# Loads and stores of 90-row tiles cut into a block of 64 rows at partition 32 and a small rest

## The chip, the cores and the metric

The kernel runs on one core of a Trainium2 chip. The metric is the device time of one execution in microseconds; a lower time is better. A core has five engines that run their own instruction streams beside each other: TensorE (PE, with its weight loads PEld), VectorE (DVE), ScalarE (ACT), GpSimd (POOL) and SyncE (SP). Here SP does nothing but issue transfers between the chip's main memory and the on-chip memory of 128 partitions; the transfers run on sixteen DMA engines.

## The reference

A long convolution of `x` (8 batches, 5696 positions, 128 channels) with `h`, done by a Fourier transform of twice the length, is followed by a "soft mixture of experts" over all 45568 tokens:

```python
Xf = np.fft.rfft(x, n=2*S, axis=1); Hf = np.fft.rfft(h, n=2*S, axis=0)
y = np.fft.irfft(Xf * Hf[None], n=2*S, axis=1)[:, :S].reshape(B*S, D)
logits = y @ phi                                   # 32 slots
d = softmax over tokens;  slot_input = d.T @ y     # 32 x 128
slot_out = relu(slot_input @ w1[e]) @ w2[e]        # 8 experts, 4 slots each
out = softmax over slots(logits) @ slot_out
```

## The kernel before, in words

The convolution is a transform in two factors, N1 = 90 and N2 = 64, all in float32 matrix products. The 5696 positions are 89 rows (R1) of 64. The work runs in 92 steps over one list written out by hand (`for t in range(steps)`), in which four stages of different batches stand beside each other. The filter `h` goes first as group 0, then the eight batches of `x`.

- Stage A, steps 0 to 71, eight steps per group. `load_x` (L157) brings 89 rows of `x` into a tile `xc` (a ring of three), three steps ahead. `fold` (L174, POOL) adds and subtracts its two halves into `x0` and `x1`. `stage_a` (L183) multiplies by the table `s1` (L190, PE), ACT copies two results into the tile `fst` (L192, three buffers), and SP stores 90 rows of it to main memory as F (L195). There are two F stores a step.
- Stage B, from step 9. `load_g` (L201) reads F back in another order, as 128 rows, four units ahead (`gt`, five buffers; 23 units per group, three a step). PE multiplies by `wt` (L220), DVE by the transformed filter (L238 to L244), PE by `vt` (L256); ACT copies into `zst` (L259, three buffers), and SP stores it as z (L261). For the filter, ACT and DVE keep the results on the chip instead (L227 to L232). The tables `wt` and `vt` are loaded in pieces during steps 7 to 22 (L525).
- Stage C, from step 26, one pair of tiles every two steps. `load_z` (L281) reads z back as 90 rows into `zc` (a ring of two, four near the end; the two added ones are called `zd`). PE multiplies by the table `i1` (L308), DVE and POOL fold (L314 to L324), PE transposes (L331), and the logits, the running softmax over tokens and the weighted sums follow (L341 to L424). A step's softmax weights go to main memory (L452).
- The tail, after the last step: the experts, and then the output, 25 stores of up to 1 MB (L696 to L713).

SP works in program order: an F store that waits for ACT holds back all transfers after it. Its transfers use eight semaphores in turn, and each waits until the transfer eight places before it has landed.

Only part of the 128 partitions holds data in these tiles, and the tables are padded to match. `SPLIT` is 80, so an x load is one transfer of 80 rows and one of 9; the other two are single transfers of 90 rows. The offsets are constants:

```python
SPLIT = R1 // 16 * 16
Z0, X0, F0 = 20, 20, 19
```

The rest of `xc` and `zc` is set to zero once, so unused rows add nothing to a product.

Of the kernel before, what the change touches and what calls it, by code (L numbers as in the profile page):

```python
# [14 lines left out]
PSUM = bass.MemoryType.PSUM  # L15


def transform_tables(S, N1, N2, CH, Z0, X0, F0):

    N, R1, HALF, P = N1 * N2, S // N2, N2 // 2, 2 * N2
    k1 = np.arange(N1)  # L30
    alpha = np.pi * (k1 + 0.5) / N1
    m1 = np.arange(R1) - (N1 - 1) / 2
    a1 = np.outer(m1, alpha)
    s1 = np.stack([np.cos(a1), -np.sin(a1), -np.cos(a1)], 1)
    a0 = np.outer(alpha, np.arange(N1 // 2) + 0.5)
    i1 = np.stack([np.cos(a0), -np.sin(a0), -np.cos(a0)], 1)
    s1 = np.pad(s1, [(X0, P - R1 - X0), (0, 0), (F0, P - N1 - F0)])
    i1 = np.pad(i1[np.arange(N1).reshape(2, N1 // 2).T.reshape(-1)],
                [(Z0, P - N1 - Z0), (0, 0), (0, N2 - N1 // 2)])
    k2 = np.arange(N2)  # L40
    omega = np.pi * (k1[:, None] + 2 * N1 * k2[None] + 0.5) / N
    m2 = np.arange(HALF) - (N2 - 1) / 2
    a2 = m2[None, :, None] * omega[:, None, :]
    w = np.concatenate([np.cos(a2), np.sin(a2)], 1)
    NP = N1 // 2
    back = np.arange(N2).reshape(2, HALF // CH, CH).transpose(1, 0, 2).reshape(-1)
    wbd = np.zeros((2 * N2, NP, 2 * N2))
    vbd = np.zeros((2 * N2, NP, 2 * N2))
    for par in range(2):
        r = slice(par * N2, (par + 1) * N2)  # L50
        wbd[par::2, :, r] = w[par * NP:(par + 1) * NP].transpose(1, 0, 2)
        vbd[r, :, r] = w[par * NP:(par + 1) * NP][:, back].transpose(2, 0, 1)
    turn = (N1 - 1) / 2 * alpha[:, None] + (N2 - 1) / 2 * omega
    tn = np.zeros((2 * N2, 2, NP))
    for par in range(2):
        r = slice(par * N2, (par + 1) * N2)
        tn[r, 0] = np.cos(turn[par * NP:(par + 1) * NP]).T / N
        tn[r, 1] = np.sin(turn[par * NP:(par + 1) * NP]).T / N
    return [np.ascontiguousarray(t, dtype=np.float32) for t in (s1, i1, wbd, vbd, tn)]
# [3 lines left out]
def kernel(  # L63
# [24 lines left out]
    nc = tc.nc  # L88
    P = 128
    B, S, D = x.shape  # L90
# [4 lines left out]
    N1, N2 = 90, 64  # L95
    R1, HALF, NP = S // N2, N2 // 2, N1 // 2
    CH = 4
# [5 lines left out]
    HP = P // 2  # L103
    NQ = NJ // 2
    assert S == R1 * N2 and R1 == N1 - 1 and D == P and CH == Q == 4
    SPLIT = R1 // 16 * 16
    Z0, X0, F0 = 20, 20, 19
    ctx.enter_context(tc.manual_schedule())

    t_s1, t_i1, t_w, t_v, t_turn = [  # L110
        nc.inline_tensor(t, f"tab_{n}").ap()
        for n, t in zip(("s1", "i1", "w", "v", "turn"), transform_tables(S, N1, N2, CH, Z0, X0, F0))]
    fd = [nc.dram_tensor(f"f_{g}", (N2, N1, 2, D), F32, kind="Internal").ap() for g in range(B + 1)]
    zd = [nc.dram_tensor(f"z_{b}", (NP, 2 * N2, 2, D), F32, kind="Internal").ap() for b in range(B)]
    cd = nc.dram_tensor("c_t", (P, B * NQ, Q, 2, MH), F32, kind="Internal").ap()
# [7 lines left out]
    i1 = const.tile([P, 3, HP], F32, name="i1")  # L123
# [16 lines left out]
    s1 = apool.tile([P, 3, P], F32, name="s1", tag="s1", bufs=1)  # L140
    wt = fconst.tile([P, NP, P], F32, name="wt")
    vt = fconst.tile([P, NP, P], F32, name="vt")
    turn = fconst.tile([P, 2, NP], F32, name="turn")
# [3 lines left out]
    def bank():  # L147
        return ps.tile([P, 512], F32, name="bank", tag="bank")
# [8 lines left out]
    def load_x(c):  # L157
        if c >= (B + 1) * NJ:
            return
        g, j = divmod(c, NJ)  # L160
        src = (h if g == 0 else x[g - 1]).rearrange("(a n) d -> a n d", n=N2)
        t_ = xcs[c % len(xcs)]
        gap = N2 - CH * (2 * j + 1)
        for r in (slice(0, SPLIT), slice(SPLIT, R1)):
            v = src[r, CH * j:CH * (j + 1), :]
            v = bass.AP(tensor=v.tensor, offset=v.offset,
                        ap=[v.ap[0], [gap * D, 2], [1, CH * D]])
            nc.sync.dma_start(
                out=t_[X0 + r.start:X0 + r.stop, :, :, :].rearrange("p s n d -> p s (n d)"), in_=v)
        xs[c] = t_  # L170
# [12 lines left out]
    def stage_a(c, comp):  # L183
        g, j = divmod(c, NJ)
        src = folded.pop((c, comp))
        tab = (0, 1) if comp == 0 else (1, 2)
        st = apool.tile([P, CH, 2, D], F32, name="fst", tag="fst", bufs=3)
        for G in range(2):
            p = bank()
            nc.tensor.matmul(p[:, :], s1[:, tab[G], :],  # L190
                             src[:, :, :].rearrange("p n d -> p (n d)"), start=True, stop=True)
            nc.scalar.activation(st[:, :, G, :],  # L192
                                 p[:, :].rearrange("p (n d) -> p n d", d=D), AF.Copy)
        n0 = comp * HALF + CH * j
        nc.sync.dma_start(out=fd[g][n0:n0 + CH, :, :, :].rearrange("n k g d -> k n (g d)"),  # L195
                          in_=st[F0:F0 + N1, :, :, :].rearrange("k n g d -> k n (g d)"))


    gs, prods = {}, {}
# [81 lines left out]
    def load_z(c):  # L281
        b, j = divmod(c, NJ)
        t_ = zring.pop(0)
        zring.append(t_)
        w_ = 2 * CH * 2 * D
        nc.sync.dma_start(
            out=t_[Z0:Z0 + N1, :, :, :, :].rearrange("k o n c d -> k (o n c d)"),
            in_=zd[b].rearrange("q (a r) c d -> (q a) (r c d)",
                                a=2)[:, j * w_:(j + 1) * w_])
        zs[c] = t_  # L290

    def load_pair(T):
        if T < NT:
            load_z(2 * T)
            load_z(2 * T + 1)
# [186 lines left out]
    loaded = 0  # L482

    load_x(0)
    nc.scalar.dma_start(out=s1[:, :, :], in_=t_s1)
    for c in range(1, 3):
        load_x(c)
# [8 lines left out]
    for t in range(steps):  # L496
# [31 lines left out]
        if t < NA:  # L528
            load_x(t + 3)
            stage_a(t, 0)  # L530
            fold(t + 1, 0)
# [16 lines left out]
        if t < NA:  # L548
            stage_a(t, 1)
            fold(t + 1, 1)  # L550
# [13 lines left out]
        if t == last_front:  # L564
# [5 lines left out]
            for i in range(2):  # L570
                t_ = last.tile([P, 2, CH, 2, D], F32, name=f"zd{i}")
# [7 lines left out]
        if e > 0:  # L579
            if landed:  # L580
                place_all(*landed.pop(0))
            if kept:
                n = min(NQ, len(kept))
# [3 lines left out]
        if 0 <= i < E // 2:  # L587
            nc.sync.dma_start(
                out=w2s[:, 2 * i:2 * i + 2, :, :],
                in_=moe_w2[2 * i:2 * i + 2].rearrange("e (p c) d -> p e c d", p=P))  # L590
# [6 lines left out]
    for q in range(Q):  # L597
        r = slice(q * NSL, (q + 1) * NSL)
        nc.vector.tensor_copy(out=rep4[r, :, :],
                              in_=ident[r, r].unsqueeze(1).broadcast_to([NSL, Q, NSL]))  # L600
    p = bank()
# [5 lines left out]
    p = bank()  # L607
# [7 lines left out]
    p = bank()  # L615
# [8 lines left out]
    p = bank()  # L624
# [12 lines left out]
    for g in range(EG):  # L637
        for f0 in range(0, F, FH):
            p = bank()
# [4 lines left out]
            src = p[:, :].rearrange("p (c k) -> p k c", k=NFC)  # L644
# [5 lines left out]
    for g in range(EG):  # L650
        for k0 in range(0, NFC, 4):
            p = bank()
            for k in range(4):
# [3 lines left out]
                out=hidT[:, g, k0:k0 + 4, :], in_=p[:, :].rearrange("p (k c) -> p k c", k=4))  # L657
# [9 lines left out]
    p = bank()  # L667
# [18 lines left out]
    for b in range(B):  # L686
        for w0 in range(0, NV, G4):
            n = min(G4, NV - w0)
# [10 lines left out]
            for q in range(Q):  # L699
                dst = o_[:, 0:n + lone, q, :]  # L700
                src = pq[q][:, 0:(n + lone) * D].rearrange("p (k d) -> p k d", d=D)
# [6 lines left out]
                out=ov[b, t0:t0 + n * RW * N2, :].rearrange("(w p n) d -> p w (n d)", p=P, n=CH),  # L708
                in_=o_[:, 0:n, :, :].rearrange("p w q d -> p w (q d)"))
            if lone:  # L710
                nc.sync.dma_start(
                    out=ov[:, NV * RW * N2:, :].rearrange("b (j n) d -> b j (n d)", n=CH),
                    in_=o_[:, n, :, :].rearrange("p q d -> p (q d)"))  # L713
# [29 lines left out]
```

## Time and profile before

| what | value |
|---|---|
| median of 4 runs | 1124.95 us (1119.29 to 1127.17) |
| the profiled execution | 1119.29 us, its span 1117.4 us |
| busy: PE, PEld, DVE, ACT, POOL | 980.1, 614.6, 718.4, 517.1, 365.7 us |
| DMA engines | 78.0% busy for the main queue, 247 GB/s mean |
| mean granted TensorE clock | 0.943 |
| F stores / x loads / z loads | 144 of 360 KB / 72 of 320 KB and 72 of 36 KB / 64 of 720 KB |

The profile is one execution, taken by the hardware profiler. Busy time counts an engine's work, not its waiting; its share is a mean over stages with different limits. The chain follows the work that ended last back through what released each step, and so tells which engine or transfer set the time. A stretch's row gives the busy time of each engine between two times, the granted clock, the mean busy share of the sixteen DMA engines and GB/s. In SP's rows, the duration is the issue of a transfer alone; its landing comes later.

### The profile page before, as it was taken

The page shows a single profiled execution, that of the slowest core. Times are in us where ns is not written, and L with a number is a line of the kernel's source. Part 1 is how long each engine was busy: PE and PEld are TensorE (multiplying, and loading weights), DVE is VectorE, ACT ScalarE, POOL GpSimd, SP SyncE. Part 2 cuts the span into 40 slices and gives each one's busy share as a digit, 9 for nine tenths or more (in the row PEclk, how much of TensorE's full clock was granted, in tenths as well). Part 3 has the DMA queues.
Part 4 walks back from the last instruction along what each step waited for, and adds up shares of the span by engine and source line. Part 5 has one row for each costly group of instructions (what it writes and reads, how often), then busy time and mean ns, then how long its engine had stood idle before and what let it go on. Part 6 is the DMA issues. An engine that isn't in the chain of part 4 may idle for free.

```text
span 1117.4 us, 17250 instructions
## 1 busy us (share of the span) xinstructions
PE 980.1 (88%) x5690; PEld 614.6 (55%) x5690; DVE 718.4 (64%) x1384; ACT 517.1 (46%) x1049; POOL 365.7 (33%) x340
## 2 busy tenths in 40 slices
PE   7688898999999999999999999999997888686884
PEld 2354565555555555555555555555554555354683
DVE  2044565677777767776777677767777878565442
ACT  4477344445545444554555444444443333244332
POOL 5433222333333333333333333333331112276000
PEclk9899899999999999999999999999999999787855
DMA  7999898978788777777787778877776775764399
GB/s 204 301 275 278 290 325 267 307 252 258 231 254 252 242 232 246 250 243 231 240 248 249 232 236 249 254 227 242 246 222 190 250 253 170 210 201 164 121 381 339
DMA packets 175110, 275.49 MB, mean 247 GB/s; under 512 B 12864, under 2 KB 115776, under 8 KB 169263
## 3 DMA queue, kind: packets, MB, share of 16 engines
q1 hardware_dynamic: 174447, 274.04, 78.0%
q8 instruction: 46, 0.75, 0.3%
q10 hardware_dynamic: 576, 0.36, 0.1%
q14 instruction: 41, 0.34, 0.1%
HBM read 145.95 MB, written 128.39 MB: 246 GB/s over the span
## 4 chain that ended last, share of the span: by engine, by line
PE 65%; DVE 19%; DMA 10%; issue 2%; ACT 1%; SPq 1%; POOL 1%; DVEq 0%; ACTq 0%; POOLq 0%
PE bank L190 16%; PE bank L256 12%; PE bank L220 11%; PE bank L308 11%; PE bank L331 6%; DVE y L324 4%; DMA out_dram<-o 4%; DMA gt<-f 3%; DVE y L323 3%; PE ap L417 3%; PE bank L341 2%; DVE om L315 2%; DVE op L314 2%; DVE pi L238 2%; DVE pr L238 2%
## 5 line engine op out<-in xcount | busy, mean ns | idle before, releaser
L179 POOL TENSOR_TENSOR x<-xc 128x512 f32<-128x512 f32 x144 | 187.1, 1300 | 336.6 <-PE bank L190 314.8
L190 PE MATMUL bank<-x,s 128*128 128x512 f32 x576 | 276.8, 609 | 7.8 <-POOL x L179 7.8
L259 ACT ACTIVATE zst<-bank 128x512 f32<-128x512 f32 (+1 forms) x184 | 108.3, 588 | 347.0 <-PE bank L256 278.6
L256 PE MATMUL bank<-yf,vt 128*128 128x256 f32 x720 | 190.1, 386 | 67.3 <-DVE yf L244 63.0
L220 PE MATMUL bank<-gt,wt 128*128 128x256 f32 x810 | 220.7, 395 | 18.8 <-DMA gt<-f 18.5
L220 PEld LDWEIGHTS bank<-gt,wt 128*128 128x128 f32 x810 | 145.6, 192 | 114.1 <-issue 50.3
L192 ACT ACTIVATE fst<-bank 128x512 f32<-128x512 f32 x288 | 168.5, 598 | 72.7 <-PE bank L190 57.9
L238 DVE TENSOR_TENSOR pr<-bank,Hr 128x512 f32<-128x512 f32 (+1 forms) x184 | 124.2, 675 | 109.1 <-PE bank L220 109.1
L256 PEld LDWEIGHTS bank<-yf,vt 128*128 128x128 f32 x720 | 134.2, 191 | 102.3 <-issue 71.2
L190 PEld LDWEIGHTS bank<-x,s 128*128 128x128 f32 x576 | 108.9, 194 | 95.9 <-issue 62.9
L238 DVE TENSOR_TENSOR pi<-bank,Hi 128x512 f32<-128x512 f32 (+1 forms) x184 | 122.8, 667 | 0.0
L308 PE MATMUL bank<-zc,i 128*64 128x512 f32 x480 | 118.7, 610 | 3.9 <-DMA zc<-z 3.9
L242 DVE TENSOR_TENSOR yf<-pr,pi 128x256 f32<-128x256 f32 (+1 forms) x184 | 78.5, 427 | 6.4
L406 POOL TENSOR_TENSOR L<-L,rs 128x512 f32<-128x512 f32 x32 | 33.5, 1048 | 133.3 <-DVE rs L405 133.3
L331 PE MATMUL bank<-ident,y 128*128 128x128 f32 x512 | 69.0, 294 | 9.2 <-DVE y L324 9.2
L244 DVE TENSOR_TENSOR yf<-pr,pi 128x256 f32<-128x256 f32 (+1 forms) x184 | 75.8, 412 | 0.0
L351 DVE TENSOR_REDUCE mx<-lt 64x1 f32<-64x360 f32 x64 | 33.2, 518 | 64.4 <-ACT lt L345 63.5
L331 PEld LDWEIGHTS bank<-ident,y 128*128 128x128 f32 x512 | 65.0, 154 | 13.3 <-issue 10.6
L332 ACT ACTIVATE yt<-bank 128x360 f32<-128x360 f32 x128 | 56.2, 471 | 34.6 <-PE bank L331 34.6
L229 DVE SCALAR_TENSOR_TENSOR Hr<-bank,turn,pr 128x128 f32<-128x128 f32 x45 | 15.7, 349 | 74.3 <-ACT pr L227 74.3
L308 PEld LDWEIGHTS bank<-zc,i 128*64 128x64 f32 x480 | 29.6, 137 | 55.6 <-issue 53.5
L378 POOL MEMSET dt<- 64x8 f32 x32 | 3.4, 106 | 173.4 <-ACT dn L381 98.6
(97 smaller groups left out, 997.9 us busy)
## 6 DMA issues: line engine op xcount, KB each, us to landing
f<-fst SPq DMA_DIRECT2D x144, 360.0 KB
gt<-f SPq DMA_DIRECT2D x198, 256.0 KB
z<-zst SPq DMA_DIRECT2D x176, 256.0 KB
zc<-z SPq DMA_DIRECT2D x60, 720.0 KB
xc<-in_x_dram SPq DMA_DIRECT2D x64, 320.0 KB
out_dram<-o SPq DMA_DIRECT2D x16, 1024.0 KB
out_dram<-o SPq DMA_DIRECT2D x8, 768.0 KB
c_t<-cst SPq DMA_DIRECT2D x26, 180.0 KB
```

What stands on the lines that cost most here:

```text
L179: nc.gpsimd.tensor_tensor(out=y_[:, :, :], in0=t_[:, 0, :, :], in1=t_[:, 1, ::-1, :], op=AL.subtract if comp else AL.add)
L190: nc.tensor.matmul(p[:, :], s1[:, tab[G], :], src[:, :, :].rearrange("p n d -> p (n d)"), start=True, stop=True)
L192: nc.scalar.activation(st[:, :, G, :], p[:, :].rearrange("p (n d) -> p n d", d=D), AF.Copy)
L220: nc.tensor.matmul(p[:, q * 256:(q + 1) * 256], wt[:, 2 * i + q, :], t_[:, q, :, :].rearrange("p c d -> p (c d)"), start=True, stop=True)
L238: nc.vector.tensor_tensor(out=t[:, 0:n, :, :], in0=pv[:, 0:n, :, :], in1=H[:, 2 * i:2 * i + n, :].unsqueeze(2).broadcast_to([P, n, 2, D]), ...
L242: nc.vector.tensor_tensor(out=y_[:, 0:n, 0, :], in0=pr[:, 0:n, 0, :], in1=pi[:, 0:n, 1, :], op=AL.subtract)
L244: nc.vector.tensor_tensor(out=y_[:, 0:n, 1, :], in0=pr[:, 0:n, 1, :], in1=pi[:, 0:n, 0, :], op=AL.add)
L256: nc.tensor.matmul(p[:, q * 256:(q + 1) * 256], vt[:, 2 * i + q, :], y_[:, q, :, :].rearrange("p c d -> p (c d)"), start=True, stop=True)
L259: nc.scalar.activation(st[:, 0:n, :], p[:, 0:n * 256].rearrange("p (q c) -> p q c", q=n), AF.Copy)
L308: nc.tensor.matmul(p[h_ * HP:(h_ + 1) * HP, :], i1[:, tab, :], t_[:, o, :, q, :], start=True, stop=True)
L331: nc.tensor.transpose(p[:, i * P:(i + 1) * P], ys[T][:, k * CH + i, 0:D], ident[:, :])
L332: nc.scalar.activation(yt[:, k * CH:(k + 1) * CH, :, :], p[:, :].rearrange("p (n h r) -> p n h r", n=CH, h=2)[:, :, :, 0:MH], AF.Copy)
```

## The change

Three kinds of transfer are cut differently, and the rows of the tiles are placed differently; the bytes moved and the arithmetic are the same.

- An x load puts rows 0 to 63 at partitions 32 to 95, rows 64 to 87 at 96 to 119 and row 88 at 120, as three transfers (64, 24 and 1 rows).
- The table `s1` puts F's rows 0 to 63 at partitions 32 to 95 and rows 64 to 89 at 6 to 31, and F is stored from there by two transfers (64 and 26 rows).
- A z load puts rows 0 to 63 at partitions 32 to 95 and rows 64 to 89 at 0 to 25, by two transfers. The rows of the table `i1` are permuted to match.

```diff
-def transform_tables(S, N1, N2, CH, Z0, X0, F0):
+def transform_tables(S, N1, N2, CH, X0, frows, zrows):
...
-    s1 = np.pad(s1, [(X0, P - R1 - X0), (0, 0), (F0, P - N1 - F0)])
-    i1 = np.pad(i1[np.arange(N1).reshape(2, N1 // 2).T.reshape(-1)],
-                [(Z0, P - N1 - Z0), (0, 0), (0, N2 - N1 // 2)])
+    part = s1
+    s1 = np.zeros((P, 3, P))
+    for a, b, p in frows:
+        s1[X0:X0 + R1, :, p:p + b - a] = part[:, :, a:b]
+    part = i1[np.arange(N1).reshape(2, N1 // 2).T.reshape(-1)]
+    i1 = np.zeros((P, 3, N2))
+    for a, b, p in zrows:
+        i1[p:p + b - a, :, :N1 // 2] = part[a:b]
...
-    SPLIT = R1 // 16 * 16
-    Z0, X0, F0 = 20, 20, 19
+
+    X0, BLOCK = 32, 64
+    frows = ((0, BLOCK, 32), (BLOCK, N1, 32 - N1 + BLOCK))
+    zrows = ((0, BLOCK, 32), (BLOCK, N1, 0))
+    xrows = (slice(0, BLOCK), slice(BLOCK, R1 - 1), slice(R1 - 1, R1))
...
-        for r in (slice(0, SPLIT), slice(SPLIT, R1)):
+        for r in xrows:
...
-        nc.sync.dma_start(out=fd[g][n0:n0 + CH, :, :, :].rearrange("n k g d -> k n (g d)"),
-                          in_=st[F0:F0 + N1, :, :, :].rearrange("k n g d -> k n (g d)"))
+        for a, b, p in frows:
+            nc.sync.dma_start(
+                out=fd[g][n0:n0 + CH, a:b, :, :].rearrange("n k g d -> k n (g d)"),
+                in_=st[p:p + b - a, :, :, :].rearrange("k n g d -> k n (g d)"))
...
-        nc.sync.dma_start(
-            out=t_[Z0:Z0 + N1, :, :, :, :].rearrange("k o n c d -> k (o n c d)"),
-            in_=zd[b].rearrange("q (a r) c d -> (q a) (r c d)",
-                                a=2)[:, j * w_:(j + 1) * w_])
+        src = zd[b].rearrange("q (a r) c d -> (q a) (r c d)", a=2)
+        for k, e_, p in zrows:
+            nc.sync.dma_start(out=t_[p:p + e_ - k, :, :, :, :].rearrange("k o n c d -> k (o n c d)"),
+                              in_=src[k:e_, j * w_:(j + 1) * w_])
```

More of the change, by code (lines that the diff above doesn't have):

```diff
@@ L111 @@
         nc.inline_tensor(t, f"tab_{n}").ap()
-        for n, t in zip(("s1", "i1", "w", "v", "turn"), transform_tables(S, N1, N2, CH, Z0, X0, F0))]
+        for n, t in zip(("s1", "i1", "w", "v", "turn"), transform_tables(S, N1, N2, CH, X0, frows, zrows))]
     fd = [nc.dram_tensor(f"f_{g}", (N2, N1, 2, D), F32, kind="Internal").ap() for g in range(B + 1)]
```

## The prediction

> **What bounds the kernel now.** I read the page first, then its chain, the chain in order of time for the first 140 us, the stretches, SP's rows in one period, and last the landings of every transfer (the trace keeps each transfer's issue and, engine by engine, its arrivals).
>
> ```profile
> DMA  7999898978788777777787778877776775764399
> q1 hardware_dynamic: 174447, 274.04, 78.0%
> PE 65%; DVE 19%; DMA 10%; issue 2%; ACT 1%; SPq 1%; POOL 1%; DVEq 0%; ACTq 0%; POOLq 0%
> 25.00:50.00 25.00, 18.41 (x43) 7.03 (x41) 0.00 (x0) 12.70 (x24) 14.76 (x12) 0.94 0.96 291
> 75.00:100.00 25.00, 20.45 (x67) 11.70 (x66) 11.82 (x40) 17.64 (x54) 8.51 (x7) 1.00 0.96 296
> 300.00:400.00 100.00, 95.69 (x513) 58.77 (x512) 73.19 (x138) 49.56 (x96) 34.52 (x32) 1.00 0.83 257
> 435.00:453.00 18.00, 18.00 (x116) 11.66 (x116) 11.61 (x25) 9.31 (x19) 4.92 (x4) 1.00 0.99 307
> 453.00:463.00 10.00, 8.57 (x35) 5.06 (x32) 9.19 (x15) 4.56 (x10) 5.11 (x5) 1.00 0.47 150
> ```
>
> The chain is PE and DVE; transfers hold only 10% of it, while the sixteen transfer engines are busy 78% of the span. The stretches (us, then busy time of PE, PEld, DVE, ACT, POOL, granted clock, DMA share, GB/s) say where those 10% lie. Up to 115 us the engines are full (0.96) and PE waits. From 140 us on PE is the bound: of a 28 us period the transfers fill 18 us and leave the last 10 us half empty.
>
> ```profile
> 24.45 4.02 DMA f<-fst
> 28.58 1.09 ACT fst L192 x2
> 29.69 0.34 SPq L195
> 30.12 0.45 SPq L168
> 30.62 0.97 SPq L168
> 31.68 4.20 DMA f<-fst
> ...
> 70.71 5.84 DMA gt<-f
> 956.78 8.49 DMA zc<-z
> ```
>
> In the chain (start, length, what) the filling phase has two halves. Until 47 us a cycle of two steps is: an F store lands, ACT refills the tile, SP issues F and two x loads, the next F store lands. From 52 to 115 us, eight steps of some 7.6 us, each ends in a G load of 5.6 to 6.1 us. After 115 us one transfer is left on the chain before the output: z at 956 us.
>
> ```profile
> 520.19 0.80 SPq L286 DMA_DIRECT2D zc<-z  x2
> 521.09 0.97 SPq L168 DMA_DIRECT2D xc<-in_x_dram  x2
> 522.15 0.32 SPq L195 DMA_DIRECT2D f<-fst  x1
> 522.53 0.48 SPq L207 DMA_DIRECT2D gt<-f  x1
> SPq L261 <- DMA zc<-z: 18.6, 10, 2.4
> SPq L261 <- ACT zst L259: 312.3, 142, 5.2
> ```
>
> SP issues everything in program order, 0.3 to 0.5 us a transfer. Its semaphores for transfers are eight, used in turn, so that transfer n waits for the landing of transfer n-8; the wait of a z store for z loads (18.6 us in all) is that, not data.
>
> **The change part by part.** The sum is made against the profiled execution, 1119.29 us (span 1117.4), the fastest of four; the median is 1124.95, and what the sum adds is carried over to it.
>
> *What moves.* The bytes stay. An x load is three transfers instead of two (72 more), an F store two instead of one (144), a z load two instead of one (64 loads, four of them the zd lines): 280 more on SP. The landings show how rows become engines: 80 or 128 rows land on 16, 90 on 15, 9 on 9, each engine with equal rows: the largest divisor up to 16. By that 64 rows take 16, 26 take 13, 24 take 12, and the lone row its two pieces on 2. So the fullest engine carries what it did: of F 6 rows before, 4+2 now; of z the same; of x 5+1 before, 4+2 now, and on two engines one packet more. The trace does not number the engines; that small transfers use the same first ones is assumed. A gain from spreading is therefore not in the sum.
>
> *Packets.* F's 1024-byte packets take 54.0 ns at 20 to 47 us, most of them 46; x's 2048-byte ones 109, most of them 84; z's 8192-byte ones 494 ns (300 to 700 us), the fastest eighth near 309. If the blocks of 64 ran at the fastest value and the rests too, a filling step would save at most 48x8 ns + 12x25 ns = 0.7 us on an engine, over 17 steps 12 us. The other end is the added x packet, 0.11 us a step, 2 us in all. Most F packets are at the floor already, so I take 0.
>
> [...]
>
> *Filling, first half (9 steps to 47 us).* Per two steps the chain gains the second F part twice (0.34+0.05 each) and the third x load (0.36+0.05): 1.2 us, 0.6 a step, 5.4 in nine. Against it: the x issue that took 0.97 and 1.42 us takes 0.36 where nothing presses, so 0.6 us or more of it is waiting for full queues and gives way; and an F store takes 3.30 us unloaded (at 12 us) against 4.0 to 4.5 here. With engines at 0.96 little is left to lose: 0.15 a step, +1.3; ends -0.5 (a shorter F) and +5.4.
>
> *Filling, second half (8 steps to 115 us).* SP runs without a pause from 67.23 to 73.2 us: F, gt, wt, x, x, F, gt, gt. Three added issues (two of 0.39, one 0.41) put the second G load 1.2 us later. The weight load's issue of 1.22 us is 0.32 unpressed, which covers 0.9; the G load lands 5.84 us after issue where a lone one took 2.86, so a later issue loses queueing first. Eleven transfers a step instead of eight also make the eight semaphores bind: the second G load now waits for the F part issued eight before it, some 0.9 us. Both lie beside full queues: +0.1 a step, +1; ends 0 and +9.6. If the cover goes (queues drained), the G load at the step's end is late next, and PE behind it.
>
> *Steady periods, 115 to 950 us: nothing.* Added are nine or ten issues a period, 4 us of SP. The burst z, x, F now has nine transfers (4+3+2), so the second F part waits for the first z part, and G load, z store and logits store behind it leave up to 3 or 4 us later. What hides it, read as landing to first use at 400 to 700 us: G at least 7.0 us, x 18.8, the F tile's refill 10.8, a z pair 5.0, the z tile's refill 2.1. Moreover over a megabyte stays in flight, and landings follow the engines (0.99 busy), not the issue. The z store has the least cover; past 2.1 us ACT's refill at L259 is late, then PE at L256. Lower end: z loads that shrink open no wait, since none is on the chain: 0.
>
> *Added waits.* Each matmul pair at L308 waits for two more semaphores, 2x32 in all; a semaphore row on SP takes 17 ns: +1.1 us on PE; 0 if they pass during the matmul before. POOL's fold and ACT's refill get one or two each, in engines that idle half the time: nothing; without that idle time some 290x17 ns = 5 us.
>
> *The z load at 956 us.* The pair lands 8.9 us after its first issue. Six packets per engine and tile at 485 ns are 2.9 us; four at 309 and two at 485 are 2.2, so -1.4 for the pair; two added issues at most +0.8. I take -0.3.
>
> Sum: 0 + 1.3 + 1.0 + 0 + 1.1 - 0.3 = +3.1 us, that is 1122.4 for an execution like the profiled one, and **1128** beside the median.
>
> **The rivals.**
> - *Issue bound in the filling (slower).* SP's added 0.6 us in nine steps and 1.2 in eight are exposed: +15, 1140 us. For it: F and x issues already stand on the chain, and eight semaphores for eleven transfers. Against: full engines. It decides once DMA's share in 52 to 115 us falls below about 0.85 (a step's 7.6 us growing by 0.8).
> - *Late z stores (slower).* The burst after a z load delays a z store's landing by 3 us instead of none: over 2.1 us of cover, about 1 us per pair, 29 pairs: 1154 us. For it: the smallest margin of all; against: landing follows the engines.
> - *Faster packets (faster).* F and x packets come down in the filling by two thirds of the 12 us, and the 956 us wait by 1.4: -9.4, with the 3.4 us of issue and waits +3.4: -6, 1119; at the whole -13 and nothing lost, 1112. For it: z and x packets are far above their fastest; against: F's are not.
>
> [...]
>
> **How the numbers follow.** About 0.5% (5.6 us) is what a measurement here tells from no change. Forecast (1119.5 to 1130.5, within 0.5%): 0.55. Issue bound 0.20 and late z stores 0.07 make 0.27 slower. Faster packets: 0.18. One in ten left out at each side gives 1115 to 1142: it reaches over the whole issue-bound case and half of the fast one.
>
> **What would show it.** Right: 1109 transfers on SP where 829 were; DMA share in 25 to 100 us still 0.93 or more; the G wait ending the first phase within 3 us of 114; steady periods of 28.1 us with L308 not waiting; "under 512 B" packets (one per transfer and engine) up by some 3,300 from 12,864. Packet means of F, x and z tell the alignment: unchanged within 5% for F, z between 370 and 490 ns. Wrong: a DMA share that falls while the filling grows (issue bound); ACT's L259 waiting for z stores in every period (late z stores); the first phase ending 8 us early (faster packets).

## The result and the profile after

The changed kernel takes 1128.31 us (median of 51 runs, 1122.07 to 1135.62), the kernel before 1122.56 us on the same chips (77 runs, 1116.00 to 1128.52). The ratio is 1.0048 [1.0038, 1.0058]: slower by 5.4 us (4.3 to 6.5), as the means of the executions have it; the medians lie 5.75 us apart. The forecast was 3.1 us over before. Sign and size are near, but the terms of the sum are not: one grew to more than four times its size.

The page of the kernel after (its profiled execution took 1126.74 us): the span, the DMA share in 40 slices, the packets, SP's queue, the chain's shares.

```profile
span 1124.9 us, 17617 instructions
DMA  6888999987788787877778778777876675664399
DMA packets 178376, 275.53 MB, mean 245 GB/s; under 512 B 16127, under 2 KB 119039, under 8 KB 172526
q1 hardware_dynamic: 177710, 274.05, 77.0%
PE 64%; DVE 20%; DMA 8%; issue 2%; ACT 2%; SPq 2%; POOL 1%; DVEq 0%; ACTq 0%; POOLq 0%
```

The span grew by 7.5 us. In the second to fourth slices (28 to 112 us) the DMA share fell from 9 tenths to 8. On the chain SP's own issuing went from 1% to 2% and transfers from 10% to 8%: the chain holds less moving and more issuing. Packets under 512 B rose by 3,263, near the 3,300 that the prediction has for the 280 added transfers (one per transfer and engine).

The stretches of the kernel after (us; busy time of PE, PEld, DVE, ACT, POOL; granted clock, DMA share, GB/s):

```profile
25.00:50.00 25.00, 19.24 (x43) 7.23 (x41) 0.00 (x0) 10.59 (x20) 14.12 (x12) 1.00 0.84 250
50.00:75.00 25.00, 16.21 (x45) 10.24 (x46) 6.52 (x22) 11.91 (x34) 5.59 (x5) 0.73 0.83 266
75.00:100.00 25.00, 21.00 (x67) 12.07 (x66) 11.62 (x40) 18.01 (x54) 7.60 (x6) 1.00 0.93 297
300.00:400.00 100.00, 95.71 (x538) 60.17 (x531) 72.31 (x139) 49.80 (x96) 35.02 (x31) 1.00 0.82 252
```

From 25 to 50 us the transfer engines were busy 0.96 of the time, and now are 0.84; from 75 us on they are nearly as full as before (0.93 against 0.96), and at 300 to 400 us PE is as busy as it was. The loss is in the first half of the filling phase. The time from the issue of the first F store to the last landing of the first G load, called the filling time below, was 40.04 us (12.28 to 52.32) and is 45.79 us (12.39 to 58.18): +5.75. After that little is added: the first stage C pair starts 3.9 us later than before, the 24th 4.1 us, so 640 us of steady periods add 0.2 (28.08 and 28.10 us a period from the third pair on). The 3.9 is less than 5.75: the first product on the second group's G is still 6.0 us late at 114 us, and then the execution profiled before had TensorE's clock halved for 6.8 us at 115 us, and this one had not.

The chain of the kernel after, in order of time (start, length, what), in the filling's first half and at z:

```profile
45.93 0.61 ACT fst L201
46.54 0.22 SPq L205
46.81 0.57 SPq L205
47.38 0.06 issue
47.48 0.59 SPq L205
48.11 3.26 DMA f<-fst
51.48 1.09 ACT fst L201 x2
...
53.01 0.57 SPq L205
53.58 0.06 issue
53.68 0.59 SPq L205
54.32 0.58 SPq L205
54.94 3.23 DMA gt<-f
...
965.92 6.66 DMA zc<-z
```

In place of an F store's one row of 0.34 us stand two of 0.57 to 0.59, and the next store's two stand behind them. The F landing behind them is shorter than before (3.26 us; it was 4.0 to 4.2). The part is smaller, but that alone is not it: in fz60 below, whose first F part has 60 rows and whose engines stay nearly as busy as before, that part lands in 4.3 us (median at 20 to 47 us), against 3.3 for the 64 rows here. The engines' queues are emptier (0.84 of the time busy, 0.96 before), which can be read as SP no longer filling them. SP's own rows in one filling stretch (start, us, line, what, count), before:

```profile
25.79 0.32 SPq L195 DMA_DIRECT2D f<-fst  x1
26.20 1.88 SPq L168 DMA_DIRECT2D xc<-in_h_dram  x2
28.18 1.85 SPq L195 DMA_DIRECT2D f<-fst  x2
30.12 1.47 SPq L168 DMA_DIRECT2D xc<-in_x_dram  x2
31.68 1.90 SPq L195 DMA_DIRECT2D f<-fst  x2
```

and after:

```profile
27.84 1.87 SPq L205 DMA_DIRECT2D f<-fst  x3
29.81 1.44 SPq L177 DMA_DIRECT2D xc<-in_h_dram  x3
31.35 2.50 SPq L205 DMA_DIRECT2D f<-fst  x4
33.95 1.91 SPq L177 DMA_DIRECT2D xc<-in_x_dram  x3
35.97 2.54 SPq L205 DMA_DIRECT2D f<-fst  x4
38.60 1.91 SPq L177 DMA_DIRECT2D xc<-in_x_dram  x3
40.62 1.21 SPq L205 DMA_DIRECT2D f<-fst  x2
```

A row's length covers its pauses: before, two F issues of 0.34 us span 1.85 us, since SP waits for ACT between them. After, four F issues fill 2.50 us, and each row begins 0.1 us behind the last: SP never pauses in this stretch. By line, with the shortest, median and longest issue in ns, of the kernel before and then of the kernel after:

```profile
L195 SPq DMA_DIRECT2D f<-fst x144: 317/338/422, 12.3 to 839.3; - x144
```
```profile
L205 SPq DMA_DIRECT2D f<-fst x288: 396/583/1494, 12.4 to 844.0; - x144
```

Twice as many issues, each 1.7 times as long. The prediction had twice as many at the old length.

### The profile page after: what moved, and what is told of

The parts are those of the page before. It is cut to its first block, busy times and chain, and to the rows that moved or that the text cites. A ratio compares the mean times of both kernels' runs of the same rounds, so it can differ in the third digit from the quotient of the medians.

```text
span 1124.9 us, 17617 instructions
## 1 busy us (share of the span) xinstructions
PE 976.0 (87%) x5690; PEld 609.4 (54%) x5690; DVE 719.9 (64%) x1384; ACT 517.2 (46%) x1049; POOL 365.3 (32%) x340
## 4 chain that ended last, share of the span: by engine, by line
PE 64%; DVE 20%; DMA 8%; issue 2%; ACT 2%; SPq 2%; POOL 1%; DVEq 0%; ACTq 0%; POOLq 0%
PE bank L199 15%; PE bank L267 12%; PE bank L319 11%; PE bank L231 10%; PE bank L342 5%; DVE y L335 4%; DVE y L334 3%; DMA out_dram<-o 3%; PE ap L428 3%; PE bank L352 2%; DVE pr L249 2%; DVE pi L249 2%; DVE om L326 2%; DVE op L325 2%; DMA xc<-in_x_dram 2%
## 5 line engine op out<-in xcount | busy, mean ns | idle before, releaser
L319 PE MATMUL bank<-zc,i 128*64 128x512 f32 x480 | 120.5, 616 | 6.0 <-DMA zc<-z 6.0
L342 PE MATMUL bank<-ident,y 128*128 128x128 f32 x512 | 65.0, 283 | 10.3 <-DVE y L335 10.3
L342 PEld LDWEIGHTS bank<-ident,y 128*128 128x128 f32 x512 | 60.8, 147 | 14.2 <-issue 11.4
L319 PEld LDWEIGHTS bank<-zc,i 128*64 128x64 f32 x480 | 30.0, 139 | 59.7 <-issue 56.5
```

Of the source, the lines that this page charges most:

```text
L319: nc.tensor.matmul(p[h_ * HP:(h_ + 1) * HP, :], i1[:, tab, :], t_[:, o, :, q, :], start=True, stop=True)
L342: nc.tensor.transpose(p[:, i * P:(i + 1) * P], ys[T][:, k * CH + i, 0:D], ident[:, :])
```

## The experiments

Three theories were put to the runs. *Time of issue*: SP has hardly a pause left in the first half, and what counts is how long its issues take. *Count*: an added transfer costs by being one more, whatever its issue takes (its place in the queue, its semaphore). *Packets*: starting partitions and spreading change how long packets take. What separates the first two is that the length of an issue can be changed apart from the count: at 20 to 47 us F's 90 rows take 0.32 us before and its 64 rows 0.60 after (medians), and the lone row's x load takes 0.65 us after, but 0.25 in the one step of eight in which its two pieces of 2 KB join. b60 and b80 keep the count with other rows, and plain makes the issues long with the count of before.

One table holds what the runs showed. "Issues" and "SP us" are SP's transfers and its time in issue per step, from the first F issue of step 2 to that of step 7; an issue's time is the whole length of its row, which can include standing still (the same x load of before took 0.31 us at 9 us and 1.65 at 113 us). "Pause" is the sum of SP's gaps of over 0.15 us between issues in the same steps. DMA is the share at 20 to 35 and 35 to 50 us. Rows of F, x and z are in the order of their transfers. All but the ratio are from one profiled execution each; a ratio is from 5 (plain), 6 (b80, relief), 8 (x_only) or 12 executions, and 51 of after, against 17 to 77 of before.

| kernel | F | x | z | issues | SP us | pause us | filling us | DMA | ratio to before |
|---|---|---|---|---|---|---|---|---|---|
| z60_only | 90 | 80+9 | 60+30 | 4.2 | 2.27 | 1.46 | 38.9 | 0.93, 0.98 | 0.9983 [0.9965, 1.0001] |
| z_only | 90 | 80+9 | 64+26 | 4.2 | 2.49 | 1.19 | 40.0 | 0.92, 0.97 | 0.9994 [0.9969, 1.0019] |
| before | 90 | 80+9 | 90 | 4.2 | 2.52 | 1.18 | 40.0 | 0.94, 0.97 | 1 |
| align | 90 | 80+9 | 90 | 4.2 | 2.21 | 1.61 | 40.2 | 0.94, 0.98 | 1.0006 [0.9981, 1.0030] |
| fz60 | 60+30 | 80+9 | 60+30 | 6.2 | 2.58 | 1.13 | 40.3 | 0.92, 0.96 | 0.9971 [0.9951, 0.9991] |
| x2row | 60+30 | 60+27+2 | 60+30 | 7.2 | 3.46 | 0.50 | 41.3 | 0.87, 0.90 | 0.9998 [0.9977, 1.0019] |
| f_only | 64+26 | 80+9 | 90 | 6.2 | 3.76 | 0.13 | 42.5 | 0.89, 0.94 | 1.0011 [0.9985, 1.0037] |
| b60 | 60+30 | 60+28+1 | 60+30 | 7.2 | 3.74 | 0.25 | 43.2 | 0.88, 0.88 | 1.0016 [0.9992, 1.0039] |
| plain | 90 | 80+9 | 90 | 4.2 | 3.76 | 0.46 | 44.1 | 0.87, 0.91 | 1.0124 [1.0095, 1.0153] |
| x60_only | 90 | 60+28+1 | 90 | 5.2 | 3.62 | 0.53 | 44.6 | 0.86, 0.87 | 1.0026 [1.0005, 1.0048] |
| x_only | 90 | 64+24+1 | 90 | 5.2 | 3.56 | 0.59 | 44.6 | 0.90, 0.91 | 1.0070 [1.0043, 1.0097] |
| after | 64+26 | 64+24+1 | 64+26 | 7.2 | 4.13 | 0.11 | 45.8 | 0.85, 0.82 | 1.0048 [1.0038, 1.0058] |
| b80 | 80+10 | 80+8+1 | 80+10 | 7.2 | 4.30 | 0.10 | 46.0 | 0.84, 0.86 | 1.0091 [1.0060, 1.0123] |
| relief | 64+26 | 64+24+1 | 64+26 | 5.0 | 2.94 | 1.47 | 46.4 | 0.70, 0.88 | 1.0572 [1.0535, 1.0609] |

The four kernels that issue F and x as before, without plain's switch, fill in 38.9 to 40.2 us, which shows how far one execution may be off. They and fz60 pause for 1.1 to 1.6 us a step; all that lose filling time, relief aside, for 0.6 us or less. Down the table the ratio rises on the whole with the filling time, by roughly 1 us for each us of filling (5.4 for 5.75 in the kernel after), but loosely: x_only and x60_only fill in the same time and differ by 0.4%. Where it rises more (plain, b80, x_only), more is lost later, which the profiles below show.

**Nothing but a switch: plain.** The kernel before, with one switch of the language. What it alters in an instruction is not shown; what it does to the issues is.

```
+    nc.dge_precook = False
```

> [...] Theory 2: the number of transfers is unchanged, so nothing, +0. [...]

Measured: 1.0124 [1.0095, 1.0153], 13.9 us, more than three times what the first theory had: the author's estimate for it took some 0.6 us, as of the 64 rows, for every issue, and came to +1 to +4 us. Same transfers, same bytes, same partitions; F's issue is 0.87 us where it was 0.34, and not 0.6:

```profile
L196 SPq DMA_DIRECT2D f<-fst x144: 845/870/896, 13.2 to 851.2; - x144
```

The filling grows by 4.1 us and the DMA share falls to 0.87, near the 0.85 of the kernel after. The count is that of the kernel before, so without any added transfer longer issues can do this. Another 6 to 7 us are lost at 190 to 212 us, where the first pair of z loads comes late; no z transfer stands there on the chain before or after:

```profile
195.88 4.19 DMA z<-zst
...
201.16 8.29 DMA zc<-z
```

**The same count with blocks of 60: b60.** The kernel after with 60 rows in place of 64.

```
-    X0, BLOCK = 32, 64
+    X0, BLOCK = 32, 60
```

> The changed kernel with blocks of 60 rows instead of 64: F 60+30, z 60+30, x 60+28+1. As many transfers as the changed kernel (1109 on SP), the same first partition 32, the same six rows on the fullest engine. Theory 1, SP's issue time: in the changed kernel a 64-row transfer takes 0.59 us to issue and the one behind it 0.56, so that a step of the filling needs 4.5 us of SP where the transfers need 3.8; if that is a matter of the number 64, the issues here are 0.33 to 0.40, a step needs about 2.9 us of SP, and the 5.9 us that the changed kernel loses by 58 us fall to 0 to 1; in all +0 to +1.5 us on before (ratio 1.000 to 1.0015). Theory 2, the number of transfers and the eight semaphores: as slow as the changed kernel, +5 us (1.0045). Theory 3, packets: as the changed kernel, with z packets near 430 ns.

Measured: 1.0016 [0.9992, 1.0039]. F's two parts are issued in 0.36 and 0.45 us (medians at 20 to 47 us) in place of 0.60 and 0.57, and the filling time is 43.2 us: of +5.75 a good half, 3.2, stays, 2.6 goes. In the median the difference to before is no longer told from nothing. Neither theory has it all: 2.6 us go with the 64-row issues, the rest is left with 7.2 issues a step.

**Another division: b80.** The same with 80 rows.

```
-    X0, BLOCK = 32, 64
+    X0, BLOCK = 32, 80
```

> The changed kernel with blocks of 80 rows: F 80+10 (80 at 32 to 111, 10 at 22 to 31), z 80+10 (10 at 0), x 80+8+1. As many transfers as the changed kernel, the block on sixteen engines as with 64 rows. Theory 1: 80 rows have the short issue, so the filling loses 0 to 1 us; +0 to +1.5 us in all, which separates the number 64 from the number of engines. Theory 2: +5 us. [...]

Measured: 1.0091 [1.0060, 1.0123]. In the median the slowest of the pure divisions and above both times expected (up to 1.5 and 5 us), though F's issues are shorter than in the kernel after (0.39 us in the median of all, 0.58 there). A gain over the kernel after, as the issue time would give, did not come. F's 10-row part takes 0.44 us in the median but up to 1.64, the 80-row x load 0.95, so SP's time rises to 4.30 us a step all the same. By an estimate from the landings before and after (90 rows on 15 engines, 80 on 16; 64 on 16, 26 on 13, 24 on 12), the fullest engine gets 5 and 1 rows of F and z here, where 60 and 30 give it 4 and 2. Later the z loads are late here too (z packets mean 544 ns at 300 to 700 us, 494 before); the profiled execution, at 1138.01 us, is the slowest of the six and 7 us above their median, so it may show more of this than the others:

```profile
203.93 7.22 DMA zc<-z
225.39 9.17 DMA zc<-z
234.62 3.88 DMA z<-zst
```

**Only F: f_only.** F in 64 and 26 rows, x and z as before.

```
-    X0, BLOCK = 32, 64
+    X0, BLOCK = 20, 64
...
-    zrows = ((0, BLOCK, 32), (BLOCK, N1, 0))
-    xrows = (slice(0, BLOCK), slice(BLOCK, R1 - 1), slice(R1 - 1, R1))
+    zrows = ((0, N1, 20),)
+    xrows = (slice(0, R1 // 16 * 16), slice(R1 // 16 * 16, R1))
```

> The change made for F stores alone (64 rows at partition 32 and 26 at 6); x loads stay 80+9 at 20, z loads 90 at 20. 144 added transfers. Theory 1: a filling step has four F issues of 0.6 and two x issues of 0.36 to 0.5, with gaps 3.4 to 3.7 us of SP against 3.8: near the edge, so +1 to +3 us. Theory 2, in proportion to the added transfers (144 of 280): +2.8 us, with the loss partly after 58 us.

Measured: 1.0011 [0.9985, 1.0037], filling +2.5 us.

**Only x: x_only.** x in 64, 24 and 1 rows, F and z as before.

```
-    frows = ((0, BLOCK, 32), (BLOCK, N1, 32 - N1 + BLOCK))
-    zrows = ((0, BLOCK, 32), (BLOCK, N1, 0))
+    frows = ((0, N1, 19),)
+    zrows = ((0, N1, 20),)
```

> The change made for x loads alone (64, 24 and 1 rows from partition 32); F stores stay 90 rows at 19, z loads 90 at 20. 72 added transfers. Theory 1: a filling step has 0.6+0.56+0.65 for x and two F of 0.33 to 0.57, 2.5 to 3.0 us of SP against 3.8: hidden, 0 to +0.7 us, so that the losses of F alone and x alone do not add up to the changed kernel's. Theory 2: 72 of 280, +1.4 us.

Measured: 1.0070 [1.0043, 1.0097], 7.9 us, above both expectations (0 to 0.7 and 1.4 us); filling +4.6 us. With one added issue a step x costs more than F with two. Some is lost after the filling: the first stage C pair starts 3.2 us later than before, the second 5.3. The parts do not add up: 2.5 and 4.6 make 7.1, both together 5.75.

**Only x with a block of 60: x60_only.** As x_only, in 60, 28 and 1 rows.

```
-    X0, BLOCK = 32, 64
+    X0, BLOCK = 32, 60
```

> Only x split, into 60, 28 and 1 rows, F and z in one transfer each. With x alone in 64, 24 and 1 rows the period was 4.47 us, the first use of G +4.6 us, the ratio 1.0070. If the time of the issues decides: x parts of 0.40, 0.40 and 0.57 us instead of 0.61, 0.56 and 0.65, 3.1 us of issue a step instead of 3.56, period 4.1 to 4.2 us, first use of G +1.5 to +2.5 us, ratio 1.001 to 1.003. If the third x load or the lone row costs by itself (its place in the queue, its two engines): 4.4 to 4.5 us, +4 to +5 us, ratio 1.005 to 1.007.

Measured: 1.0026 [1.0005, 1.0048], less than x_only in the median; but the filling takes the same 44.6 us and the period of steps 2 to 7 is 4.49 us, as the count would have it. The x issues did not become shorter: in the median 1.19 us for 60 rows and 1.04 for 28 (20 to 47 us), up to 1.56, where b60's shortest rows of that kind are near 0.4. They can be read as issues that stand still at a full queue, where 60 rows are worth nothing. This leaves something open: the engines are busy only 0.86 of the time here, and SP still pauses 0.53 us a step, so not all queues can be full. By the same estimate the transfers land on different numbers of engines (60 rows on 15, 28 on 14; the lone row lands on 2 in the kernel after), and one engine's queue may be fuller than another's; the traces do not number the engines, and no run settles it. After the filling x60_only loses less than x_only: its second stage C pair starts 3.6 us later than before, where x_only's starts 5.3 us later.

**F and z in 60 and 30 rows, x as before: fz60.**

```
-    X0, BLOCK = 32, 64
+    X0, BLOCK = 32, 60
...
-    xrows = (slice(0, BLOCK), slice(BLOCK, R1 - 1), slice(R1 - 1, R1))
+    xrows = (slice(0, R1 // 16 * 16), slice(R1 // 16 * 16, R1))
```

> F and z as 60 rows at partition 32 and a rest of 30, x in two transfers of 80 and 9 rows as before (at partition 32). If the time of the issues decides: F parts of 0.35 and 0.44 us (as in the blocks of 60) add 0.9 us a step to 2.5, which leaves SP pauses, so the period is 4.0 to 4.1 us, the first use of G +0.5 to +1.5 us, the ratio 0.998 to 1.001. If the count decides: 6.2 issues a step as with F alone in 64 and 26 rows, so 4.33 us, +2.6 us and a ratio of 1.001 to 1.003.

Measured: 0.9971 [0.9951, 0.9991], and a filling time of 40.3 us: nothing lost with two more issues a step, DMA share 0.92 and 0.96.

```profile
20.00:35.00 15.00, 15.00 (x36) 5.92 (x35) 0.00 (x0) 8.73 (x17) 11.00 (x9) 1.00 0.92 285
35.00:50.00 15.00, 8.79 (x21) 3.15 (x19) 0.00 (x0) 6.30 (x13) 7.59 (x6) 0.91 0.96 283
```

Against f_only, with as many issues of F, the period of steps 2 to 7 falls from 4.33 to 4.04 us: for F a second transfer a step costs nothing that shows; the long issues of 64 and 26 rows do. The two divisions differ in one thing more, which no run separates: 64 and 26 rows land on 16 and 13 engines in the kernel after, 60 and 30 on 15 each by the estimate above. This version beats both kernels, before by 0.1 to 0.5%. Where that gain lies its profile does not show: its filling is not shorter, and its profiled execution ended later than the one of before. Among a dozen intervals one that just misses 1 can also be chance.

**Three x loads, none of one row: x2row.** As b60, but the rest of x in 27 and 2 rows.

```
-    xrows = (slice(0, BLOCK), slice(BLOCK, R1 - 1), slice(R1 - 1, R1))
+    xrows = (slice(0, BLOCK), slice(BLOCK, R1 - 2), slice(R1 - 2, R1))
```

> Blocks of 60 in all three (F and z 60 and 30 rows), x in 60, 27 and 2 rows: against the blocks of 60 with x in 60, 28 and 1 rows only the last load differs, against F and z in 60 and 30 with x in 80 and 9 rows there is a third x load. From the first F store to the landing of the first G load it was 40.0 us before, 43.2 with 60, 28 and 1, and 40.3 with 80 and 9. If the lone row's long issue (0.58 us, where loads of two pieces otherwise take 0.36 to 0.41 unpressed) makes the difference: issue 0.35 to 0.45 us, 40.5 to 41.5 us, period of steps 2 to 7 of 4.05 to 4.2 us instead of 4.41, ratio 0.997 to 1.000. If a third x load costs whatever its issue (its place in the queue and among the eight semaphores): 42.8 to 43.6 us, period 4.4 us, ratio 1.001 to 1.003.

Measured: 0.9998 [0.9977, 1.0019], filling 41.3 us, both inside the ranges of the first answer. The last load's issue falls from 0.57 to 0.26 us. But the period of steps 2 to 7 hardly moves (4.33 from 4.41), as the second answer has it; most of the 1.9 us is gained in steps 0 to 2. So from b60 to fz60 the 2.9 us divide into about 1.9 for the lone row and 1.0 for a third x load, with single executions half a us unsure. That it is the lone row's issue is likely but not shown: the middle load changed too, from 28 rows to 27.

**A second queue: relief.** The kernel after, with the 26-row part of F issued by ACT.

```
-        for a, b, p in frows:
-            nc.sync.dma_start(
+        for (a, b, p), queue in zip(frows, (nc.sync, nc.scalar)):
+            queue.dma_start(
```

> The kernel after, with the second F part (26 rows) issued by ACT instead of SP; nothing else is changed, all 1109 transfers stay. If SP's issue time makes the loss: SP's issue time a step in steps 2 to 7 falls from 4.13 us by two F rests (about 1.1 us) to 3.0, pauses of SP come back, the period falls from 4.71 us to 4.2 or less, the first use of G comes 1.5 to 3.5 us later than before instead of 5.9, and the ratio is 1.000 to 1.003. If the number of transfers makes it, wherever they are issued: period 4.7 us, first use of G +6, ratio 1.005. If ACT's refills suffer from the added issues (two of 0.6 us a step beside some 2 us of copies): as late or later, ratio 1.005 or more.

Measured: 1.0572 [1.0535, 1.0609], 64 us, more than ten times what any theory had; only the third, with its open end, covers it, and its cause is not the one found. SP's issue time did fall, from 4.13 to 2.94 us a step, and its pauses came back (1.47 us a step in place of 0.11), but they are waits. SP's waits in the steady part, 300 to 600 us (for whom: us, times, longest):

```profile
SPq L218 <- DMA f<-fst: 34.2, 8, 6.9
SPq L272 <- DMA f<-fst: 33.3, 9, 5.7
SPq L205 <- DMA f<-fst: 29.5, 7, 5.8
SPq L463 <- DMA f<-fst: 11.6, 5, 3.5
```

In the kernel after no F store stands in that list's first rows; there SP waits for ACT's z tiles. The two queues share the eight semaphores, in the order of the program: SP's last issue before 388 us ends at 387.42, and its next is a G load at 394.42, on the semaphore that ACT's F part, issued only at 392.45, gave back on landing at 394.36. SP thus waits for an issue that ACT has not come to yet, with all its queue behind it. As a test of the issue time the run says nothing, for the new wait hides it.

**Only z: z_only and z60_only.** z in 64 and 26 rows, and in 60 and 30, F and x as before.

```
-    X0, BLOCK = 32, 64
-    frows = ((0, BLOCK, 32), (BLOCK, N1, 32 - N1 + BLOCK))
+    X0, BLOCK = 20, 64
+    frows = ((0, N1, 19),)
...
-    xrows = (slice(0, BLOCK), slice(BLOCK, R1 - 1), slice(R1 - 1, R1))
+    xrows = (slice(0, R1 // 16 * 16), slice(R1 // 16 * 16, R1))
```

(z60_only has 60 in place of 64.)

> The change made for z loads alone (64 rows at partition 32 and 26 at 0); x and F as before. 64 added transfers, none in the filling. Theory 1: the filling as before (0 by 115 us); z packets fall from 490 to about 430 ns as in the changed kernel; the wait for z near 956 us, 8.9 us from its first issue to the landing of the pair before and 10.7 in the changed kernel, stays long because four issues of 0.5 stand where two were: +0 to +2 us in all. Theory 2: 64 of 280, +1.2 us. Theory 3 (shorter z packets help): -1 us.

> z loads alone, cut into 60 rows at partition 32 and 30 at 0, x and F as before. As many transfers as with 64 and 26. Theory 1: issues of 0.33 to 0.42, so the wait near 956 us is shorter than with 64 rows by about 0.5 us: -0.5 to +1 us. Theory 2: +1.2 us, as with 64 rows.

Measured: 0.9994 [0.9969, 1.0019] and 0.9983 [0.9965, 1.0001]. No cost of the added z issues shows in these two, long or short; the intervals leave room for at most some 2 us.

**Only the partition: align.** One F store, one z load, x in 80 and 9 rows, all from partition 32 on.

```
-    frows = ((0, BLOCK, 32), (BLOCK, N1, 32 - N1 + BLOCK))
-    zrows = ((0, BLOCK, 32), (BLOCK, N1, 0))
-    xrows = (slice(0, BLOCK), slice(BLOCK, R1 - 1), slice(R1 - 1, R1))
+    frows = ((0, N1, 32),)
+    zrows = ((0, N1, 32),)
+    xrows = (slice(0, R1 // 16 * 16), slice(R1 // 16 * 16, R1))
```

> The partitions moved and nothing cut: F, z as one transfer of 90 rows at partition 32, x as 80+9 rows at 32. No transfer is added. Theories 1 and 2: 0 us. [...]

Measured: 1.0006 [0.9981, 1.0030]. The packets of z (8192 B, 300 to 700 us) take 510 ns on average, 494 before: the starting partition alone does nothing that shows.

## Why the prediction came out as it did

The forecast was near in part by luck, not because its terms were right. Four terms missed, by +4.4, -0.9, -0.9 and +1.5 us; with what the profiles show in their place the sum would be 7, not 3.1, and the measured 5.4 lies between. That 1128 was forecast and 1128.31 measured is luck too: the base of four executions, 1124.95, lies 2.4 us above the median of 77.

*Packets, taken as 0: right.* F's packets are at 54.4 ns (54.0 before) and x's at 112 (109), unchanged as forecast. z's fell from 494 to 434 ns, inside the 370 to 490 given. In z_only they are 464, in align 510, so it takes the division and not the partition. No time follows: F's and x's do not move, and z waits on the chain only at 956 us.

*Filling, first half, +1.3 us with ends -0.5 and +5.4: wrong (5.75, beyond the upper end), and the step that failed is its price per issue.* It took 0.34 us for a second F part and 0.36 for the third x load, from issues of 90, 80 and 9 rows. The parts measure 0.59 and 0.57 for F, 0.61, 0.56 and 0.65 for x. SP's issue time thus rises by 1.61 us a step. The prediction was right that the x issues of 0.97 and 1.42 us held waits that would give way: the 64-row and 24-row loads now take 0.61 and 0.56 with no row above 0.61 at 20 to 47 us. But it took the full queues as cover to the end (0.15 of 0.6 us a step). SP's pauses were 1.18 us a step, less than the 1.61 added: once they were used up (0.11 left) the queues ran empty (0.96 to 0.84), and the rest was exposed. Plain shows that longer issues without an added transfer do it; fz60 shows that a second F part of 0.47 us beside a first of 0.32 is still hidden.

*Filling, second half, +1.0: hidden, as was said.* The first product on G starts 5.9 us late and the first one on the second group's G 6.0: +0.1 for eight steps. A step takes 7.79 us before and 7.81 after. A cost of the eight semaphores, which the forecast named here, does not show.

*Steady periods, 0: right.* 28.08 and 28.10 us a period; SP's waits for z tiles at L272 shrank, since SP comes later to them. The waits of L319, +1.1 on PE: too much. PE's sequencer has 92 semaphore rows there in place of 61, each of 51 ns, but in 21 periods all added waits together cost some 0.2 us.

*The z load at 956 us, -0.3 with ends -1.4 and +0.8: wrong in sign.* From the pair's first issue to its last landing it took 8.88 us before and 10.65 after. Five kernels with z in one transfer (before, align, f_only, x_only, x60_only) take 8.9 to 10.2 us there (mean 9.4), six with two (after, z_only, z60_only, fz60, b60, x2row) 9.85 to 11.7 (mean 10.65), so about +1.2, with ranges that overlap. The prediction let the packets shrink; they did (418 against 485 ns at 860 to 950 us), but the pair is now issued in four transfers, whose first went out at 961.93 us, 3.1 us ahead of the rest, which waited for a z store's landing.

*The sum.* 5.75 in the filling, some 1.2 at z and 0.2 in the steady part make 7; measured are 5.4 (4.3 to 6.5). Where the 1.7 between goes stays open: filling and z are from single executions, which differ by over 1 us where F and x are issued as before. The profiled execution has 7.5, of which some 3 belong to TensorE's clock, halved for 3.4 us twice more at 860 to 920 us than in the execution profiled before. Such stretches fell elsewhere in the other profiles: fz60's profile is 2.1 us ahead of before's at 844 us and 7.2 behind at the end, while its median is the lower one.

*The rivals.* The issue-bound rival is what happened, in the first half only and at a third of its price (5.75 of 15): its second half did not come, and DMA's share in 52 to 115 us fell from 0.93 to 0.87, not below the 0.85 at which it was to decide. Late z stores did not occur; faster packets occurred for z and gave nothing. The marks: 1109 transfers on SP, the packet count and the period came as said; a DMA share of 0.93 or more from 25 us on and a first phase ending within 3 us of 114 did not (0.84 and 0.83; 120.0), and they pointed at the right rival.

The two parts of F land on average 3.2 and 3.0 us after the start of their issues (20 to 47 us), where one transfer took 4.65: what stands one behind the other is their issue on SP, 0.60 and 0.57 us.

## What to carry to other kernels

Before a transfer is split, look at the issuing engine's rows in the stage that waits for transfers: if its pauses (here 1.2 us a step) are not clearly larger than the added issues (1.6), the split can empty the queues that seemed to hide it, as here from 0.96 busy to 0.84. Price each part by an issue of the same shape and not by the mean of the line; here 60 rows cost 0.32 to 0.36 us and 64 rows 0.59. And before a second issuing queue is taken, look where its transfers stand in the turn of the completion semaphores: in relief they stood between the first queue's, and it was 64 us slower than before.

## What was not expected of the hardware

- A transfer of 64 rows is issued in 0.59 us and one of 60 rows in 0.32 to 0.36 (F), and a lone row of two pieces in 0.57 to 0.65 us where two rows take 0.26. Where the lone row's pieces join, its load takes 0.25 us, and with plain's switch F's 90 rows take 0.87 us. What makes these issues long is not shown.
- An issue's length does not go by its own rows alone: the 26-row part of F takes 0.57 us right behind the 64-row part, 0.32 and 0.33 us where SP paused between the two (twice in f_only), and 0.30 when ACT issues it. What lengthens it behind a 64-row issue was not tried.
- The issue row of a transfer is also longer where much is in flight, which can be read as a full queue: in the kernel before the same 80-row x load takes 0.31 us at 9 us (DMA share 0.13 at 8 to 10 us) and 1.65 us at 113 us (1.01 at 110 to 115 us). The landing lies outside the row: F stores of 90 rows, issued in 0.32 us, land 4.65 us after the start of their issue on average (20 to 47 us).
